# wk loaded in halves, and the last group's softmax sums on VectorE in fp32

## Chip, cores and metric

The kernel runs on one core of one Trainium2 chip. The metric is the device time of one execution in microseconds (us); for a kernel it is the median of several executions. The hardware profiler also took one execution apart, and all spans, durations and waits below come from that one.

## What is computed

A transformer block with conditioning, on 2048 rows of 512 features in bf16. Attention looks back at eight positions, every second one; the feed-forward part is gated by a GELU.

```python
mod = (silu(c) @ w_mod)                       # six vectors of 512: sa, ca, ga, sb, cb, gb
h = layernorm(x) * (1 + ca) + sa
q, k, v = split(h @ wqkv)                     # 32 heads of 16
idx = pos[:, None] - 2 * arange(8)[None, :]   # 8 keys behind each row; a negative index is masked
logits = einsum('bhsd,bhswd->bhsw', q, k[idx]) * 16 ** -0.5
attn = softmax(logits, axis=-1)               # over the 8 positions
o = einsum('bhsw,bhswd->bhsd', attn, v[idx])
x = x + ga * (o @ wo)
h = layernorm(x) * (1 + cb) + sb
x = x + gb * ((gelu(h @ w_gate) * (h @ w_up)) @ w_down)   # inner width 1792
```

## The kernel before

The 2048 rows are worked through in five groups (`GROUPS`): two of 256 rows and three of 512, numbered 0 to 4. Each group passes through `ln1` (first layer norm and its transposition into hT), `emit_qkv` (products with wq, wk, wv into PSUM, cast by ScalarE into qT, kT, vT), `emit_attention` and `emit_ffn`. The cast v rows are stored into a DRAM scratch (`scr`, L708) and read back in a layout with four shifted copies (`vR`, L725), because the sum over positions needs v by head and shift.

In attention a partition holds one head and one of four positions (128 = 4 x 32 heads), and an index `wg` of 2 in the free dimension makes eight of them. VectorE multiplies q with shifted k (`pq`, L764); TensorE folds the 16 features of a head into logits (`LT`, L776) with a 0/1 matrix. The maximum over the eight positions is taken by VectorE. For the groups 0 to 3 it is subtracted by a product (L824); for the group in `DVEMAX`, group 4, VectorE spreads it over the four partition quarters (L804) and subtracts it in fp32 in PSUM (L813). ScalarE writes the exponentials into `e` (L831). The sums over the eight positions come from two products with the matrix `F1` into a PSUM tile `ss` (L839): F1 adds the four quarters and puts the sum back into all four of them, and the two products add the two halves of e. ScalarE inverts the sum in place as exp(-ln(ss)) (L844, L845), and VectorE multiplies e by it (L848). Then come the products with vR (`pv`, L860 and L866), their fold into `o_ps` (L879), the projection with woP (`x_ps`, L904), the second layer norm, and the transposition into h2T, by DMA for all groups but group 0, followed by a modulation on ScalarE (L597).

The feed-forward part makes pairs of `g_ps` and `u_ps` (L945), 14 of them for a group of 512 rows, in a ring of four PSUM banks (`psF`) that the qkv and `y_ps` products share. ScalarE takes the GELU of the first (L954) and casts the second (L957), VectorE multiplies them (L958), and the products with WdP (`y_ps`, L971) are added to x on VectorE (L979) and stored by DMA (L982). The exponential and the GELU need different activation tables, and ScalarE loads one wherever its order changes from one to the other.

The order of the instructions is not that of the code. Each function hands its operations to a planner, `Plan`, with the engine, an estimated duration, what it reads and writes, and a priority `pri`. `Plan.order` places one operation after another: the key is the estimated start, padded by a margin of the engine (`MARGIN`) unless the engine is busy longer anyway, and among equal starts the priority decides. For loads `AHEAD` and `SKEW` stand for how far the DMA queue may run ahead and how late a transfer is seen. `emit` then issues everything in that order, so each engine works through a fixed queue. All loads, the transposing DMAs, the stores and the scr and vR transfers are issued on SyncE's (SP's) queue, in that same order. The key and the sort:

```python
if o.dma and o.pri > -996.9:
    at = max(at, pipe - self.AHEAD)
turn = self.TURN if o.eng == "pe" and o.cols != cols else 0.0
key = (max(free, at + self.MARGIN[o.eng]) + turn, o.pri)
```

The tag `prod`, six buffers, holds the pq and pv products; for the groups in `MERGE`, 3 and 4, three of the eight products lie in the buffers of wq, wk and wv. For group 0 the qkv products are cut along the contraction: wk is used in two cuts, feature blocks 0 and 1, then 2 and 3. wq is loaded in two DMAs, wk and wv in one each (L421).

Of the kernel before, what the change touches and what calls it, by code (L numbers as in the profile page):

```python
# [8 lines left out]
ACT = mybir.ActivationFunctionType  # L9
ALU = mybir.AluOpType  # L10
AX = mybir.AxisListType
F32 = mybir.dt.float32
# [6 lines left out]
def _ap(base, free_dims, offset=0):  # L19
    return bass.AP(base.tensor, base.offset + offset, [list(base.ap[0])] + [list(d) for d in free_dims])  # L20
# [164 lines left out]
class Engines:  # L185
    def __init__(self, nc, pl):
# [14 lines left out]
MERGE = (3, 4)  # L201
FMERGE = 0
DVEMAX = (4,)
CUT = 384
XB1 = {4: "act"}
XB2 = {1: "act", 2: "act", 3: "act", 4: "act"}
PRI = {
        "mod0": 3.1,
        "ln1": (-1825.3, -1417, -559.1, -142.2, 405),
        "qkv": (-441.8, 155.6, 232.8, 131.6, 1308),  # L210
        "att": (-554.3, 44.5, -1074.5, 462.1, 1752.4),
        "ffn": (1196.5, 2593, 2774.3, 2477.6, 1886.7),
        "glu": (5.6, 211.5, -2302.6, 838.6, 2147),
        "mod": (-159.3, -303.9, 262.1),
        "wo": 1823,
        "wd": 1171.4,
        "scr": -3307.9,
        "vR": -3609.4,
        "warm": (5, 6, 0, 3),
        "load": {"wk": -997.5, "wv": -995.5, "x1": -997.86, "x2": -995.23, "wm2": -1001.63, "wo": -878.5, "x3": -1000.04,  # L220
        "wm3": -994.66, "wm4": -996.59, "x4": -995.73, "Wg": -868.86, "Wu": -870.61, "wm5": -855.38, "Wd":
        -862.75},
}
Plan.MARGIN = {"pe": 0.48, "act": -0.15, "dve": 0.16, "pool": -1.48, "sp": 0.37}
Plan.AHEAD = 2.07
Plan.SKEW = 2.6
Plan.TURN = 0


# [1 line left out]
def kernel(  # L231
# [13 lines left out]
    nc = tc.nc  # L245
    P = 128
    S, D = 2048, 512
    H, DH, W = 32, 16, 8
    F = 1792
    SG = 512  # L250
    DT = D // P
# [22 lines left out]
    def ctile(shape, dtype, name):  # L274
        t = Tl(None, shape, dtype, name)
        t.t = const.tile(shape, dtype, name=name)
        return t

    T = pl.tile
    E = Engines(nc, pl)  # L280
    pe, act, dve, gp, dma = E.pe, E.act, E.dve, E.pool, E.dma
    MM = 0.2158

    def act_us(n, ptr=0):
        return 0.055 + n * 0.833e-3 + 0.093 * ptr
# [8 lines left out]
    F1 = ctile([P, P], BF16, "F1")  # L294
# [65 lines left out]
    wqkv = [T(t, [P, DT, D], BF16, t) for t in ("wq", "wk", "wv")]  # L360
    woP = T("woP", [P, 4, D], BF16, "woP")
    Wg = T("Wg", [P, DT, F], BF16, "Wg")
    Wu = T("Wu", [P, DT, F], BF16, "Wu")
    WdP = T("WdP", [P, FT, D], BF16, "WdP")
    kT = ctile([P, 4, ROW], BF16, "kT")
    scr = T("scr", [P, 4, ROW], BF16, "scr")

    def xrow(tok):
        ci = tok // P
        return xs[ci // 4][:, ci % 4, :]  # L370
# [12 lines left out]
    wm3 = T("h2T", [P, 4, D], BF16, "wm3")  # L383
    wm4 = T("h2T", [P, 4, D], BF16, "wm4")
    wm2 = [T("hh", [P, 2, D], BF16, "wm2", "early") for _ in range(2)]
    wm5 = [T("hh", [P, 2, D], BF16, "wm5", "early") for _ in range(2)]
# [17 lines left out]
    def load_rows(t, src, p, cuts, rows):  # L404
# [7 lines left out]
    L = PRI["load"]  # L412
# [3 lines left out]
        w=[wm01], pri=-999, bw=390e3)  # L416

    def load_wqkv(b, p, cuts=1):
        m = DT // cuts
        for i in range(cuts):  # L420
            dma(524e3 / cuts, lambda i=i: nc.sync.dma_start(  # L421
                out=wqkv[b][:, m * i:m * i + m, :],
                in_=A_wqkv[m * i * P:m * (i + 1) * P, b * D:(b + 1) * D].rearrange("(o p) n -> p o n", p=P)),
                w=[(wqkv[b], k) for k in range(m * i, m * i + m)], pri=p + 0.02 * i)

    load_wqkv(0, -998.65, 2)
    load_wqkv(1, L["wk"])
    load_wqkv(2, L["wv"])
    load_x(2, 4, L["x1"])
    load_x(4, 8, L["x2"])  # L430
# [1 line left out]
    for d4 in range(4):  # L432
        dma(131e3, lambda d4=d4: nc.sync.dma_start(  # L433
            out=woP[32 * d4:32 * d4 + 32, :, :],
            in_=bass.AP(A_wo.tensor, A_wo.offset + 4 * D * d4, [[16 * D, H], [D, 4], [1, D]])), w=[(woP, d4)],
            pri=L["wo"], bw=250e3)
# [31 lines left out]
    def sigmoid():  # L468
# [6 lines left out]
        w=[scT], pri=-2000)  # L475
# [72 lines left out]
    mod0 = []  # L548
# [108 lines left out]
    q, hT, vR = {}, {}, {}  # L657
# [56 lines left out]
    def emit_attention(g):  # L714
        tok0, n = GROUPS[g]
# [5 lines left out]
        for i, t in enumerate(vR[g]):  # L721
            rs = [(scr, (gg, i if GROUPS[gg][1] == SG else 0)) for gg in range(max(g - 1, 0), g + 1)]
            for r in (0, 2, 1, 3):
                queue, on = (nc.scalar, E.dma_act) if r in SECOND else (nc.sync, dma)
                on(32 * 4 * njv * (n + 8) * 2, lambda r=r, t=t, i=i, queue=queue: queue.dma_start(  # L725
                    out=t[32 * r:32 * r + 32, :, :, :].rearrange("p a b c -> p (a b) c") if njv == 4
                    else t[32 * r:32 * r + 32, :, :, :],
                    in_=bass.AP(scr.t.tensor, scr.t.offset + 2 * i * ROW + tok0 + 2 + 2 * r,
                                [[16 * ROW, H], [ROW, 16], [1, n + 8]] if njv == 4 else
                                [[16 * ROW, H], [4 * ROW, 4], [ROW, 2], [1, n + 8]])),  # L730
                    r=rs, w=[(t, r)], pri=PRI["vR"] + 0.1 * g, bw=330e3 if SECOND else 205e3)
# [8 lines left out]
        def kd(j):  # L740
            return kdep + [(kT, (bl, j)) for bl in blocks(tok0 - HALO, tok0 + n)]
# [15 lines left out]
        for jj in range(steps):  # L757
            p = base + jj
            pq = products("pq", jj)
            pqs.append(pq)  # L760
            for m in range(4):
                j, wg = (2 * jj + m // 2, m % 2) if n == SG else (m, 0)
                no = 4 if n == SG else 8
                dve(1.145, lambda j=j, wg=wg, no=no, t=pq[m]: nc.vector.tensor_tensor(  # L764
                    out=t[:], in0=_ap(q[g][:, j, :], [[0, no], [1, n]]),
                    in1=_ap(kT[:, j, :], [[2, no], [1, n]], offset=tok0 + HALO - (6 + 8 * wg if no == 4 else 14)),
                    op=ALU.mult), r=[(q[g], j)] + kd(j), w=[pq[m]], pri=p)
# [14 lines left out]
        p = base + 5  # L782
# [9 lines left out]
        e = T("e", [P, 2, n], BF16, "e")  # L792
        for b in range(nb):
            act(act_us(SG), lambda b=b: nc.scalar.copy(out=Lb[:] if nb == 1 else Lb[:, b:b + 1, :], in_=LT[b][:]),
                r=[LT[b]], w=[(Lb, b)], pri=p - 1000)
        us = 0.072 + n * 0.52e-3
        dve(us, lambda: nc.vector.tensor_tensor(out=Lb[:, 0, :], in0=Lb[:, 0, :], in1=Lb[:, 1, :], op=ALU.max),
            r=[Lb], w=[Lb], pri=p)
        if g in DVEMAX:
            mx = [T("ub", [P, n], BF16, "mx") for _ in range(2)]  # L800
# [11 lines left out]
            for b, t in enumerate(LT):  # L812
                dve(0.072 + SG * 2 // nb * 1.041e-3, lambda t=t: nc.vector.tensor_tensor(  # L813
                    out=t[:], in0=t[:], in1=_ap(all4[:], [[0, 2 // nb], [1, n]]), op=ALU.subtract), r=[t, all4], w=[t],
                    pri=p)
        else:
            dve(us, lambda: nc.vector.tensor_tensor(out=Lb[0:64, 1, :], in0=Lb[0:64, 0, :], in1=Lb[64:128, 0, :],
                                                    op=ALU.max), r=[Lb], w=[Lb], pri=p)
            dve(us, lambda: nc.vector.tensor_tensor(out=Lb[0:32, 0, :], in0=Lb[0:32, 1, :], in1=Lb[32:64, 1, :],
                                                    op=ALU.max), r=[Lb], w=[Lb], pri=p)  # L820
# [11 lines left out]

        act(act_us(SG) * nb, exps, r=LT, w=[e], pri=p - 1000, table="exp")

        ss = T("psB", [P, n], F32, "ss")

        def sums():
            for wg in range(2):
                nc.tensor.matmul(ss[:], lhsT=F1[:], rhs=e[:, wg, :], start=(wg == 0), stop=(wg == 1))  # L839

        pe(2 * MM * n / SG, sums, r=[F1, e], w=[ss], pri=p, pad=ss)

        def invert():
            nc.scalar.activation(out=ss[:], in_=ss[:], func=ACT.Ln)  # L844
            nc.scalar.activation(out=ss[:], in_=ss[:], func=ACT.Exp, scale=-1.0)  # L845

        act(2 * act_us(n) + 0.1, invert, r=[ss], w=[ss], pri=p - 1000, table="exp")
        dve(0.072 + 2 * n * 1.041e-3, lambda: nc.vector.tensor_tensor(  # L848
            out=e[:], in0=e[:], in1=_ap(ss[:], [[0, 2], [1, n]]), op=ALU.mult), r=[e, ss], w=[e], pri=p)

        oT = T("oT", [P, 4, SG], BF16, "oT")
        pvs = []
        for jj in range(steps):
            p = base + 6 + jj
            pv = products("pv", jj)
            pvs.append(pv)
            if n == SG:
                for m in range(4):
                    jl, wg = m // 2, m % 2
                    dve(1.145, lambda jj=jj, jl=jl, wg=wg, t=pv[m]: nc.vector.tensor_tensor(  # L860
                        out=t[:], in0=_ap(e[:, wg, :], [[0, 4], [1, n]]),
                        in1=vR[g][jj][:, :, jl, 8 - 8 * wg:8 - 8 * wg + n], op=ALU.mult),
                        r=[e, vR[g][jj]], w=[pv[m]], pri=p)
            else:
                for j in range(4):
                    dve(1.145, lambda j=j, t=pv[j]: nc.vector.tensor_tensor(  # L866
                        out=t[:].rearrange("p (w d) s -> p w d s", w=2), in0=_ap(e[:], [[n, 2], [0, 4], [1, n]]),
                        in1=_ap(vR[g][0][:], [[-8, 2], [njv * (n + 8), 4], [1, n]], offset=j * (n + 8) + 8),
                        op=ALU.mult), r=[e, vR[g][0]], w=[pv[j]], pri=p)

        for jj, pv in enumerate(joined(pvs)):
# [11 lines left out]
            for m, t in enumerate(o_ps):  # L883
                j = njv * jj + nj * m
                act(act_us(SG), lambda j=j, t=t: nc.scalar.copy(out=oT[:, j:j + nj, 0:n], in_=t[:]),
                    r=[t], w=[(oT, j)], pri=p - 1000)
        p = base + 11
# [3 lines left out]
        for half in range(n // 256):  # L891
# [5 lines left out]
            for i in range(2):  # L897
# [4 lines left out]
                def proj(c4=c4, x1_ps=x1_ps):  # L902
# [6 lines left out]
                    out=xrow(tok), in0=x1_ps[:], scalar=1.0, in1=xrow(tok), op0=ALU.mult, op1=ALU.add,  # L909
                    accum_out=sx[:, i:i + 1]), r=[x1_ps, xkey(tok)], w=[xkey(tok), (sx, i)], pri=p)  # L910
                act(0.7, lambda i=i, tok=tok, xn=xn, sq=sq: nc.scalar.activation(  # L911
                    out=xn[:, i, :], in_=xrow(tok), func=ACT.Square, scale=D ** -0.5, accum_out=sq[:, i:i + 1]),
                    r=[xkey(tok)], w=[(xn, i), (sq, i)], pri=p - 1000)
# [4 lines left out]
                out=rstd[:], in0=sx[:], scalar=-1.0, in1=sx[:], op0=ALU.mult, op1=ALU.mult), r=[sx], w=[rstd], pri=p2)  # L918
            dve(0.09, lambda sq=sq, rstd=rstd: nc.vector.scalar_tensor_tensor(  # L919
                out=rstd[:], in0=rstd[:], scalar=EPS, in1=sq[:], op0=ALU.add, op1=ALU.add), r=[sq, rstd], w=[rstd],  # L920
                pri=p2)
# [8 lines left out]
    def emit_ffn(g):  # L930
# [29 lines left out]
        for c4 in range(n // P):  # L960
            gc = tok0 // P + c4
            cuts = ((0, CUT), (CUT, D)) if gc == S // P - 1 else ((0, D),)
            for cut, (lo_d, hi_d) in enumerate(cuts):
# [21 lines left out]
    for g in range(NG):  # L985
        n = GROUPS[g][1]
        hT[g] = T("hT", [P, n // P, DT, P] if g in XB1 else [P, DT, n], BF16, "hT")
        ln1(g, hT[g], PRI["ln1"][g])
        if g == 0:
            mod_keep(mod0, -969)  # L990
            dve(0.34, lambda: nc.vector.tensor_copy(out=wide.t[:, 0, :].rearrange("p (t n) -> p t n", n=P),
                                                    in_=_ap(scT[:], [[1, 4], [0, P]])), r=[scT, hT[0]], w=[(wide, 0)],
                pri=-950)
        emit_qkv(g)
        if g == 0:
# [4 lines left out]
                                                       op=ALU.mult), r=[woP, (wide, 1)], w=[woP], pri=PRI["wo"])  # L1000
            for f0 in range(0, FT, 2):
                dve(0.6, lambda f0=f0: nc.vector.tensor_tensor(
                    out=WdP[:, f0:f0 + 2, :], in0=WdP[:, f0:f0 + 2, :], in1=_ap(gbB[:], [[0, 2], [1, D]]),
                    op=ALU.mult), r=[(WdP, f0), (WdP, f0 + 1), gbB], w=[(WdP, f0), (WdP, f0 + 1)], pri=PRI["wd"])
# [33 lines left out]
```

## Time and profile before

| what | value |
|---|---|
| device time, median of 5 | 243.84 us (242.17 to 244.07) |
| profiled execution, its own time | 243.5 us |
| its span, first to last instruction | 241.6 us |
| TensorE busy | 233.9 us, 1588 products |
| VectorE busy | 160.9 us |
| ScalarE busy | 159.3 us |
| GpSimd busy | 13.9 us |
| data moved by DMA | 28.23 MB |
| granted TensorE clock | 0.998 |

The busy time is per engine and the engines work side by side. PE is TensorE's multiplication, PEld its weight load, DVE is VectorE, ACT is ScalarE, POOL is GpSimd, and SPq is SyncE's queue of DMA issues. A row of a timeline gives the start, the duration, the engine, the line, the instruction with its output and inputs, and the count. A wait row gives who waited for whom, the total, how often, and the longest.

### The profile page before, as it was taken

What the parts mean: (1) busy time and instruction counts of PE and PEld (TensorE: products, weight loads), DVE (VectorE), ACT (ScalarE), POOL (GpSimd) and SP (SyncE); (2) the same over time, 40 slices, a digit from 0 to 9 for tenths busy, and PEclk for the clock granted to TensorE, in tenths of its full rate; (3) what the DMA queues carried; (4) which work ended last, traced back from release to release, by engine and by line L of the source; (5) the groups of instructions that cost most, each with busy time, mean ns of one, the idle gap of its engine ahead of it and who ended that gap; (6) DMA issues with size and microseconds to landing.
All of it is one profiled execution on the core that took longest, in us unless ns stands there. A gap on an engine that the chain in (4) does not pass through costs nothing.

```text
span 241.6 us, 4190 instructions
## 1 busy us (share of the span) xinstructions
PE 233.9 (97%) x1588; PEld 125.8 (52%) x1588; DVE 160.9 (67%) x307; ACT 159.3 (66%) x298; POOL 13.9 (6%) x35
## 2 busy tenths in 40 slices
PE   7899998999999999999999999999999999999994
PEld 2798544557674547765444444444444444444442
DVE  4689849849998699982799897589456222222222
ACT  4388785689786878579867676746867801666400
POOL 6000230000001000020000002000001000000000
PEclk9999999999999999999999999999999999999999
DMA  6999999999941129504118503200003110000011
GB/s 214 361 367 307 305 260 368 222 290 212 212 85 32 55 56 256 133 12 79 43 45 206 104 0 66 67 22 23 3 1 63 26 43 15 29 0 3 0 43 43
DMA packets 34917, 28.23 MB, mean 117 GB/s; under 512 B 10961, under 2 KB 33234, under 8 KB 34898
## 3 DMA queue, kind: packets, MB, share of 16 engines
q1 hardware_dynamic: 34896, 27.97, 46.1%
q8 instruction: 12, 0.20, 0.3%
q14 instruction: 7, 0.06, 0.1%
q10 hardware_dynamic: 2, 0.00, 0.0%
HBM read 21.40 MB, written 4.21 MB: 106 GB/s over the span
## 4 chain that ended last, share of the span: by engine, by line
PE 81%; SPq 7%; DMA 7%; DVE 2%; issue 1%; DVEq 0%
PE u_ps L945 20%; PE g_ps L945 20%; PE y_ps L971 20%; PE qkv_ps L681 8%; PE x_ps L904 6%; DMA vR<-scr 4%; DMA scr<-vT 3%; PE o_ps L879 3%; PE LT L776 3%; SPq L377 2%; DVE pv L866 1%; SPq L433 1%; SPq L395 1%; SPq L400 1%; SPq L725 1%
## 5 line engine op out<-in xcount | busy, mean ns | idle before, releaser
L945 PE MATMUL g_ps<-h2T,Wg 128*128 128x512 bf16 (+1 forms) x280 | 57.7, 337 | 0.0
L945 PE MATMUL u_ps<-h2T,Wu 128*128 128x512 bf16 (+1 forms) x280 | 57.7, 337 | 0.0
L971 PE MATMUL y_ps<-WdP,hht 128*128 128x512 bf16 (+2 forms) x238 | 50.4, 367 | 0.0
L954 ACT ACTIVATE gl<-g_ps 128x512 bf16<-128x512 f32 x56 | 33.5, 598 | 23.9 <-PE g_ps L945 19.0
L958 DVE TENSOR_TENSOR hht<-gl,ub 128x512 bf16<-128x512 bf16 x56 | 23.4, 422 | 31.0 <-ACT ub L957 30.8
L957 ACT CAST ub<-u_ps 128x512 bf16<-128x512 f32 x56 | 32.8, 585 | 15.7 <-PE u_ps L945 15.7
L945 PEld LDWEIGHTS <-Wg 128*128 128x128 bf16 x280 | 27.1, 98 | 23.3 <-issue 1.7
L945 PEld LDWEIGHTS <-Wu 128*128 128x128 bf16 x280 | 27.1, 98 | 22.2 <-issue 1.3
L764 DVE TENSOR_TENSOR pq<-qT,kT 128x2048 bf16<-128x2048 bf16 x32 | 38.0, 1217 | 0.9 <-ACT kT L704 0.9
L971 PEld LDWEIGHTS <-hht 128*128 128x128 bf16 x238 | 22.7, 98 | 25.8 <-issue 0.4
L860 DVE TENSOR_TENSOR pv<-e,vR 128x2048 bf16<-128x2048 bf16 x24 | 28.3, 1218 | 0.1
L979 DVE TENSOR_TENSOR x_sg<-y_ps,x_sg 128x512 bf16<-128x512 f32 (+2 forms) x17 | 10.8, 657 | 26.1 <-PE y_ps L971 26.1
L541 POOL TENSOR_TENSOR rstd<-rstd,neghalf 128x2 f32<-128x2 f32 x12 | 9.8, 820 | 169.5 <-DVE rstd L919 108.5
L681 PE MATMUL qkv_ps<-hT,wq 128*128 128x512 bf16 (+1 forms) x80 | 16.5, 336 | 0.7 <-ACT hT L551 0.6
L681 PE MATMUL qkv_ps<-hT,wk 128*128 128x512 bf16 (+1 forms) x80 | 16.4, 337 | 0.7 <-DMA wk<-in_A_wqkv_dram 0.7
L681 PE MATMUL qkv_ps<-hT,wv 128*128 128x512 bf16 (+1 forms) x80 | 15.5, 337 | 0.0
L904 PE MATMUL x_ps<-woP,oT 128*128 128x512 bf16 x64 | 15.3, 379 | 0.0
L911 ACT ACTIVATE xn<-x_sg 128x512 bf16<-128x512 bf16 x16 | 10.0, 627 | 4.2 <-DVE x_sg L908 4.0
L704 ACT CAST kT<-qkv_ps 128x512 bf16<-128x512 f32 x16 | 9.3, 590 | 4.4 <-PE qkv_ps L681 4.4
L620 DVE BATCH_NORM_STATS2 st<-x_sg 128x6 f32<-128x512 bf16 x16 | 10.2, 679 | 2.3 <-DMA x_sg<-in_A_x_dram 2.3
L681 PEld LDWEIGHTS <-wk 128*128 128x128 bf16 x80 | 8.7, 114 | 5.7 <-DMA wk<-in_A_wqkv_dram 1.0
L681 PEld LDWEIGHTS <-wq 128*128 128x128 bf16 x80 | 8.7, 113 | 5.3 <-issue 1.2
(100 smaller groups left out, 217.5 us busy)
## 6 DMA issues: line engine op xcount, KB each, us to landing
vR<-scr SPq DMA_DIRECT2D x24, 260.0 KB, 5.0
vR<-scr SPq DMA_DIRECT2D x8, 264.0 KB, 8.9
out_dram<-x_sg SPq DMA_DIRECT2D x15, 128.0 KB, 1.7
Wu<-in_B_w_up_dram SPq DMA_DIRECT2D x2, 896.0 KB, 10.5
scr<-vT SPq DMA_DIRECT2D x7, 256.0 KB, 7.4
Wg<-in_B_w_gate_dram SPq DMA_DIRECT2D x2, 896.0 KB, 7.8
WdP<-in_B_w_down_dram SPq DMA_DIRECT2D x2, 896.0 KB, 9.6
x_sg<-in_A_x_dram SPq DMA_DIRECT2D x3, 512.0 KB, 8.9
```

Source lines behind the costliest of these rows:

```text
L620: stats = lambda i=i, st=st, tok=tok: nc.vector.bn_stats(out=st[:, i, :], in_=xrow(tok + P * i))
L681: nc.tensor.matmul(shaped(ps[:, jl, :], g, XB1), lhsT=wqkv[b][:, dt, j + jl:D:4], rhs=columns(hT[g], g, dt, XB1), start=(dt == 0 and (jl = ...
L764: dve(1.145, lambda j=j, wg=wg, no=no, t=pq[m]: nc.vector.tensor_tensor(out=t[:], in0=_ap(q[g][:, j, :], [[0, no], [1, n]]), in1=_ap(kT[:, ...
L860: dve(1.145, lambda jj=jj, jl=jl, wg=wg, t=pv[m]: nc.vector.tensor_tensor(out=t[:], in0=_ap(e[:, wg, :], [[0, 4], [1, n]]), in1=vR[g][jj][ ...
L904: nc.tensor.matmul(x1_ps[:], lhsT=oT[:, j, c4 * P:(c4 + 1) * P], rhs=woP[:, j, :], start=(j == 0), stop=(j == 3))
L911: act(0.7, lambda i=i, tok=tok, xn=xn, sq=sq: nc.scalar.activation(out=xn[:, i, :], in_=xrow(tok), func=ACT.Square, scale=D ** -0.5, accum ...
L945: nc.tensor.matmul(shaped(ps[:, f, :], g, XB2), lhsT=Wt[:, dt, ft * P:(ft + 1) * P], rhs=columns(h2[g], g, dt, XB2), start=(dt == 0), stop ...
L954: act(act_us(SG), lambda gl=gl, ps=gu[0]: nc.scalar.activation(out=gl[:], in_=flat(ps), func=ACT.Gelu_apprx_tanh), r=[gu[0]], w=[gl], pri= ...
L957: act(act_us(SG), lambda ub=ub, ps=gu[1]: nc.scalar.copy(out=ub[:], in_=flat(ps)), r=[gu[1]], w=[ub], pri=p)
L958: dve(0.339, lambda gl=gl, ub=ub, ht=hh[u // 2], u=u: nc.vector.tensor_tensor(out=ht[:, u % 2, :], in0=gl[:], in1=ub[:], op=ALU.mult), r=[ ...
L971: nc.tensor.matmul(y_ps[:], lhsT=hh[u // 2][:, u % 2, f * n + c4 * P:f * n + (c4 + 1) * P], rhs=WdP[:, ft, lo_d:hi_d], start=(ft == 0), st ...
L979: dve(0.07 + nd * 1.041e-3, lambda y_row=y_row, y_ps=y_ps: nc.vector.tensor_tensor(out=y_row(), in0=y_ps[:], in1=y_row(), op=ALU.add), r=[ ...
```

## The change

wk is loaded by two DMAs of two feature blocks each, still as one operation of the planner. For group 4 (`DVESUM`) the two products into ss are replaced by fp32 additions on VectorE: s1 adds the two halves of e, s2 adds the upper 64 partitions to the lower 64, and four additions write the sum of both 32-partition halves of s2 to each quarter of s3. s1, s2 and s3 are fp32 tiles of the tag `prod` in SBUF. ScalarE inverts s3 in place, and e is multiplied by it. The other groups keep the products. The priorities, the margins, `AHEAD` and `SKEW` have new values.

```diff
 DVEMAX = (4,)
+DVESUM = (4,)
...
 PRI = {
-        "mod0": 3.1,
-        "ln1": (-1825.3, -1417, -559.1, -142.2, 405),
-        "qkv": (-441.8, 155.6, 232.8, 131.6, 1308),
-        "att": (-554.3, 44.5, -1074.5, 462.1, 1752.4),
-        "ffn": (1196.5, 2593, 2774.3, 2477.6, 1886.7),
-        "glu": (5.6, 211.5, -2302.6, 838.6, 2147),
-        "mod": (-159.3, -303.9, 262.1),
-        "wo": 1823,
-        "wd": 1171.4,
-        "scr": -3307.9,
-        "vR": -3609.4,
+        "mod0": 232,
+        "ln1": (-1746.8, -1408.1, -598.2, -71.1, 451.5),
+        "qkv": (-381.3, 137.8, 240.2, 131.6, 1324.9),
+        "att": (-554.3, 67.2, -1074.5, 592.2, 1636.2),
+        "ffn": (1214.9, 2614.9, 2774.3, 2238.4, 1956),
+        "glu": (-8.4, 214.5, -2060.3, 850.5, 2127.4),
+        "mod": (-285, -375.7, 388.4),
+        "wo": 1670.7,
+        "wd": 1130,
+        "scr": -3224.8,
+        "vR": -3489.3,
         "warm": (5, 6, 0, 3),
-        "load": {"wk": -997.5, "wv": -995.5, "x1": -997.86, "x2": -995.23, "wm2": -1001.63, "wo": -878.5, "x3": -1000.04,
-        "wm3": -994.66, "wm4": -996.59, "x4": -995.73, "Wg": -868.86, "Wu": -870.61, "wm5": -855.38, "Wd":
-        -862.75},
+        "load": {"wk": -997.5, "wv": -995.5, "x1": -997.86, "x2": -993.39, "wm2": -1001.63, "wo": -872.67, "x3":
+        -1000.04, "wm3": -989.07, "wm4": -995, "x4": -995.73, "Wg": -868.86, "Wu": -870.61, "wm5": -855.38,
+        "Wd": -862.75},
 }
-Plan.MARGIN = {"pe": 0.48, "act": -0.15, "dve": 0.16, "pool": -1.48, "sp": 0.37}
-Plan.AHEAD = 2.07
-Plan.SKEW = 2.6
+Plan.MARGIN = {"pe": 0.51, "act": -0.16, "dve": 0.22, "pool": -0.68, "sp": 0.23}
+Plan.AHEAD = 1.95
+Plan.SKEW = 2.48
...
-    load_wqkv(1, L["wk"])
+
+    def load_wk():
+        for i in range(2):
+            nc.sync.dma_start(out=wqkv[1][:, 2 * i:2 * i + 2, :],
+                              in_=A_wqkv[2 * i * P:2 * (i + 1) * P, D:2 * D].rearrange("(o p) n -> p o n", p=P))
+
+    dma(524e3, load_wk, w=[(wqkv[1], k) for k in range(DT)], pri=L["wk"])
...
+        if g in DVESUM:
+            add = lambda out, a, b: nc.vector.tensor_tensor(out=out, in0=a, in1=b, op=ALU.add)
+            s1, s2, s3 = [T("prod", [P, n], F32, "s%d" % k) for k in range(3)]
+
+            def spread_sums():
+                for r in range(4):
+                    add(s3[32 * r:32 * r + 32, :], s2[0:32, :], s2[32:64, :])
+
+            dve(0.6, lambda: add(s1[:], e[:, 0, :], e[:, 1, :]), r=[e], w=[s1], pri=p)
+            dve(0.6, lambda: add(s2[0:64, :], s1[0:64, :], s1[64:128, :]), r=[s1], w=[s2], pri=p)
+            dve(2.4, spread_sums, r=[s2], w=[s3], pri=p)
+
+            def invert():
+                nc.scalar.activation(out=s3[:], in_=s3[:], func=ACT.Ln)
+                nc.scalar.activation(out=s3[:], in_=s3[:], func=ACT.Exp, scale=-1.0)
+
+            act(2 * act_us(n) + 0.1, invert, r=[s3], w=[s3], pri=p - 1000, table="exp")
+            dve(0.072 + 2 * n * 1.041e-3, lambda: nc.vector.tensor_tensor(
+                out=e[:], in0=e[:], in1=_ap(s3[:], [[0, 2], [1, n]]), op=ALU.mult), r=[e, s3], w=[e], pri=p)
+        else:
...
```

More of the change, by code (lines that the diff above doesn't have):

```diff
@@ L833, in emit_attention @@
         act(act_us(SG) * nb, exps, r=LT, w=[e], pri=p - 1000, table="exp")
[L835 to L845, printed above, removed]
@@ L847, in emit_attention, with sums, invert @@
-        act(2 * act_us(n) + 0.1, invert, r=[ss], w=[ss], pri=p - 1000, table="exp")
-        dve(0.072 + 2 * n * 1.041e-3, lambda: nc.vector.tensor_tensor(
-            out=e[:], in0=e[:], in1=_ap(ss[:], [[0, 2], [1, n]]), op=ALU.mult), r=[e, ss], w=[e], pri=p)
+        if g in DVESUM:
[14 more added lines that the diff above has]
+        else:
+            ss = T("psB", [P, n], F32, "ss")
+            def sums():
+                for wg in range(2):
+                    nc.tensor.matmul(ss[:], lhsT=F1[:], rhs=e[:, wg, :], start=(wg == 0), stop=(wg == 1))
+            pe(2 * MM * n / SG, sums, r=[F1, e], w=[ss], pri=p, pad=ss)
+            def invert():
+                nc.scalar.activation(out=ss[:], in_=ss[:], func=ACT.Ln)
+                nc.scalar.activation(out=ss[:], in_=ss[:], func=ACT.Exp, scale=-1.0)
+            act(2 * act_us(n) + 0.1, invert, r=[ss], w=[ss], pri=p - 1000, table="exp")
+            dve(0.072 + 2 * n * 1.041e-3, lambda: nc.vector.tensor_tensor(
+                out=e[:], in0=e[:], in1=_ap(ss[:], [[0, 2], [1, n]]), op=ALU.mult), r=[e, ss], w=[e], pri=p)
```

## Prediction

> **What bounds the kernel now.** I read the page first, then busy time in stretches, then PE's waits, the chain of waits, and last the two places that the diff touches. The page has one row per engine, busy tenths in 40 slices, and the shares of the chain that ended last:
>
> ```profile
> PE   7899998999999999999999999999999999999994
> ...
> PE 81%; SPq 7%; DMA 7%; DVE 2%; issue 1%; DVEq 0%
> ```
>
> TensorE is full outside the first slices and carries 81% of the chain. The stretches (us, then busy us and instruction count of PE, PEld, DVE, ACT, POOL, the clock, DMA share, GB/s) say from where:
>
> ```profile
> 30.00:41.40 11.40, 9.88 (x67) 5.03 (x65) 7.78 (x12) 8.79 (x17) 2.40 (x2) 1.00 1.09 315
> 41.40:60.00 18.60, 18.59 (x159) 11.47 (x162) 14.32 (x23) 15.05 (x30) 0.69 (x1) 1.00 1.19 244
> 146.00:172.00 26.00, 26.00 (x151) 11.66 (x154) 20.82 (x33) 16.99 (x28) 1.32 (x2) 1.00 0.17 41
> 237.40:241.60 4.20, 1.09 (x16) 0.79 (x13) 1.40 (x3) 0.00 (x0) 0.00 (x0) 0.87 0.20 62
> ```
>
> From 41.4 to 237.4 us TensorE has no gap at full clock. So the time is a head of 41.4, TensorE's work behind it, and a tail of 4.2. DVE has 26 - 20.82 = 5.2 us free in the stretch with the last group's softmax. PE's waits before 41.5 us (total, times, longest):
>
> ```profile
> PE o_ps L879 <- DVE pv L866: 1.1, 2, 0.7
> PE qkv_ps L681 <- DMA wk<-in_A_wqkv_dram: 0.7, 1, 0.7
> PE qkv_ps L681 <- ACT hT L551: 0.6, 2, 0.4
> PE LT L824 <- DVE Lb L819: 0.4, 1, 0.4
> ```
>
> With two waits of 0.2 these are about 3 us, all that a better head could give after the start-up. The chain of waits (start, us, what) says what fixes the head's end:
>
> ```profile
> 16.17 0.53 SPq L433
> ...
> 16.83 8.10 DMA scr<-vT
> ...
> 27.39 9.16 DMA vR<-scr
> ...
> 40.14 1.23 DVE pv L866
> ...
> 41.41 0.40 PE o_ps L879 x8
> ```
>
> The v rows go to DRAM and back; the last pv product ends at 41.37 and releases the last fold into o_ps. That, not the early matmuls, starts the gapless stretch. The store at 16.83 stood behind two woP issues on SP's queue (to 16.70), while its last vT cast ended at 15.25 + 1.08 = 16.33.
>
> **What the Trainium skill says.** "VectorE: DVE Perf Modes", the section on the TRN2 errata, prices an fp32 tensor_tensor at (N+151)/0.96 ns, 691 at N = 512, and its tier table keeps fp32 at 1x. The trace agrees: the fp32 subtraction at L813 takes 694 ns, and L848 with 1024 elements 1214 against 1224. "TensorE: Matmul & The Clock Gate", Back-to-back issue gap, gives 518 cycles, 216 ns, for 512 columns; the two ss products take 0.43 on the chain. "DMA: Bandwidth & Descriptors", Queues, rings and completion order, says that descriptors are consumed in ring order on each DMA engine, so the first half of wk should land ahead of the second; the trace agrees as far as wk (issued 3.77, 6.8 to landing) precedes wv (4.28, 7.8).
>
> **The sums, part by part.** The parts now, from DVE's, PE's and ACT's timelines:
>
> ```profile
> 151.64 1.30 DVE L813 TENSOR_TENSOR LT<-LT,mx 128x512 f32<-128x512 f32 x2
> 155.62 0.59 PE L839 MATMUL ss<-e,F 128*128 128x512 bf16 x2
> 156.28 0.58 ACT L844 ACTIVATE ss<-ss 128x512 f32<-128x512 f32 x1
> 156.89 0.58 ACT L845 ACTIVATE ss<-ss 128x512 f32<-128x512 f32 x1
> 157.50 1.22 DVE L848 TENSOR_TENSOR e<-e,ss 128x1024 bf16<-128x1024 bf16 x1 [1.85 <-ACT ss L845]
> ```
>
> Removed: two products in the gapless stretch, 2 x 0.216 = **-0.43 us**, in full, since whatever stands behind them on PE moves up. A PSUM bank of psB comes free as well; PE never waits for one there, so nothing.
>
> Added on DVE: s1 on 128 partitions, s2 on 64, four additions on 32. Partitions do not shorten them: the max over 64 partitions takes 0.422 us, over 32 0.416. So 6 x 0.69 = 4.1 us, with overlap (the two at L813 span 1.30) some 4.0. Free DVE time there is 5.2 us, and 172 to 200 us holds 9.71 busy of 28. Ln and Exp read SBUF instead of PSUM; no row shows that on 512 fp32 elements, so 1.2 us with 0.2 either way. The last exp ends at 152.37 + 1.19 = 153.56. Then 4.0 of sums, 1.3 for the two y_ps additions (L979) that stand there, 1.2 for Ln and Exp: e is multiplied from about 160.1 instead of 157.5, **2.6 us later** (1.3 if the additions move behind). Queued behind on DVE are pv, hht and y additions; on ACT the gelu table load.
>
> Who waits? The chain to the last group's FFN: pv, o_ps at 171.7, x_ps, xn, two transposing DMAs, and the last h2T modulation ends at 190.94 + 2.22 = 193.2, before its first product at 197.7, in the middle of 56 y_ps products (190.1 to 203.9). So 4.5 us of slack as ordered, and some 9 if those products all go first. Cost of 2.6 us: nothing; without cover it is PE's time one for one.
>
> The gelu side: y_ps work of 12.1 us (56 x 0.216) starts at 147.9 and needs no gelu of group 3; it and two g/u pairs (four psF banks, 3.5 us) feed PE to 163.4. The first gelu must be done by then, so its table load (1.28 us in the trace) and gl (0.60) must start by 161.5. Inversion ends at 160.1. It fits by 1.4 us.
>
> The three prod buffers are of six; in group 4 pq and pv use only five per pass, the others lie in the finished wq, wk, wv. I find no new wait.
>
> wk: wk to wv is (4.28+7.8)-(3.77+6.8) = 1.51 us for 512 KB, so half of it lands 0.75 earlier, at 9.8, where the q products end. The four products of the first cut (0.11 each) then run during the wait, and the k products end 0.44 earlier; wv lands at 12.08 against its first product at 12.35, so 0.2 to 0.3 goes on. But the last fold still waits for pv: in the present order the gain falls into the 1.1 us of o_ps waits and nothing is left. I take **-0.2**, between -0.74 (whole wait, carried through) and +0.5 (the added issue, 0.47 to 0.51 us on SP, carried down SP's queue to the scr store). Against the latter: SP's issues from 4.84 on mostly take 0.7 to 2.4 us each, so SP is paced by DMA there, which moves the same bytes.
>
> The priorities: sorted, old and new lists of the compute stages have the same order but for mod0; the loads move wm4 alone, which must follow wm3 anyway. So the order changes by the margins, AHEAD, SKEW and the new costs, not by rank. I price it at 0, with both sides open.
>
> Sum against the profiled execution, 243.5 (span 241.6 and 1.9 around it): 243.5 - 0.43 - 0.2 = 242.9. The median of the five times is 243.84, 0.3 above it; from there **243.2**.
>
> **The rivals.** Something of about 0.5% (1.22 us) is what a measurement of this kernel can tell from no change; from 243.84 that is 242.62 and 245.06.
>
> Head re-timed for the better: the margins put the scr store ahead of a woP issue (SP's margin falls from 0.37 to 0.23) or other PE work into the waits. For: 3 us of waits stand in the head. Against: ranks are the same. Half of 2.6 us (o_ps, wk, hT; Lb is 0.4) and the 0.43: 243.84 - 1.3 - 0.43 = 242.1.
>
> Head re-timed for the worse, ending slower: the scr store falls behind one half of Wu, the next load on SP. 896 KB at 350 GB/s are 2.6 us, carried through scr, vR, pv to the fold at 41.4: 243.84 - 0.43 + 2.6 = 246.0. It decides when the store's planned time plus margin comes later than SP is free after woP; past 1.7 us of slip the result is slower than 245.06. For: vT was ready only 0.4 us before SP was. Against: the margin fell.
>
> Exp window too long: inversion past 161.5 stalls PE one for one. All four y additions and 0.2 of ACT put it at 161.7; a stall of 0.1 to 1 us: 243.5 to 244.4, no change.
>
> The change doesn't do its work: the k products wait for both halves, and the 0.43 alone stays: 243.4.
>
> **How the numbers follow.** Likeliest sum 0.42 (own range 242.6 to 243.9), halves useless 0.05, exp window 0.05 of which 0.02 slower; head better 0.31; head worse 0.17. Faster 0.31, same 0.50, slower 0.19. The range takes the likely sum and most of both head cases: 241.7 to 245.5.
>
> **What would show it.** Right: PE gapless from near 41 us, two fewer 512-column ss products, six fp32 additions of 0.69 each on DVE, gl after the inversion with no PE wait behind it, first k product near 9.9. Wrong: the last early o_ps fold far from 41.4, a PE wait on gl or hht between 155 and 200, fp32 additions of other length, or a span that moves by over 1.2 us with the head unmoved.

## The result, and the profile after

The changed kernel takes 243.73 us (median of 44 executions, 242.32 to 246.08) against 242.78 us for the kernel before (79 executions). The ratio is 1.0035, with a 95% interval of 1.0019 to 1.0050: slower by 0.46 to 1.2 us, where 0.6 faster was forecast. On a second occasion, beside variants of itself, it was 1.0003 (0.9971 to 1.0034), so the whole time alone does not settle whether the kernel got slower. The profiled execution took 243.74 us with a span of 241.8, 0.2 longer than the one before.

The page of the changed kernel, the same two rows as before:

```profile
PE   7899996999999999999999999989999999999994
...
PE 78%; DMA 9%; SPq 5%; DVE 4%; issue 2%; ACT 1%; DVEq 0%
```

Two digits changed. The 6 in the seventh slice, 36 to 42 us, was an 8: the head, where the waits for pv grew. The 8 in the 27th slice, 157 to 163 us, was a 9: TensorE has a gap where it had none, and ACT, absent from the chain before, carries 1% of it. The stretches (columns as before) put a size to the second:

```profile
41.40:60.00 18.60, 18.60 (x167) 11.54 (x163) 14.32 (x23) 15.23 (x30) 0.69 (x1) 1.00 1.17 249
146.00:172.00 26.00, 25.31 (x130) 11.26 (x122) 22.59 (x37) 17.03 (x27) 1.14 (x2) 1.00 0.17 41
```

PE is busy 25.31 us of 26; DVE rises from 20.82 to 22.59 and still has free time. PE's waits name the gap:

```profile
PE g_ps L972 <- ACT gl L981: 0.7, 1, 0.7
PE o_ps L906 <- DVE pv L893: 1.8, 3, 0.7
PE qkv_ps L688 <- DMA wv<-in_A_wqkv_dram: 0.3, 1, 0.3
```

The first row is new. The o_ps waits grew from 1.1 to 1.8, and the wait for wk, 0.7, became one of 0.3 for wv. The chain in the head (start, us, what):

```profile
17.19 7.23 DMA scr<-vT
...
26.44 9.88 DMA vR<-scr
...
39.96 1.23 DVE pv L893
...
41.23 0.40 PE o_ps L906 x8
```

The chain of the head is as before, and its end comes within 0.2 us of where it was. (The scr store is issued 0.36 us later than the 16.83 of before, and its transfer is 0.87 shorter.) The timelines of the last group's softmax on PE, DVE and ACT:

```profile
158.03 1.03 PE L972 MATMUL g_ps<-h2T,Wg 128*128 128x512 bf16 x4
158.90 1.03 PE L972 MATMUL u_ps<-h2T,Wu 128*128 128x512 bf16 x4
159.76 1.89 PE L998 MATMUL y_ps<-WdP,hht 128*128 128x512 bf16 x8
162.34 1.02 PE L972 MATMUL g_ps<-h2T,Wg 128*128 128x512 bf16 x4 [0.69 <-ACT gl L981]
```

```profile
153.49 0.69 DVE L1006 TENSOR_TENSOR x_sg<-y_ps,x_sg 128x512 bf16<-128x512 f32 x1 [0.76 <-PE y_ps L998]
154.09 0.68 DVE L843 TENSOR_TENSOR s<-e 128x512 f32<-128x512 bf16 x1
154.78 0.69 DVE L1006 TENSOR_TENSOR x_sg<-y_ps,x_sg 128x512 bf16<-128x512 f32 x1
155.50 3.55 DVE L843 TENSOR_TENSOR s<-s 64x512 f32<-64x512 f32 x5
160.41 1.23 DVE L859 TENSOR_TENSOR e<-e,s 128x1024 bf16<-128x1024 bf16 x1 [1.36 <-ACT s L856]
161.56 1.28 DVE L1006 TENSOR_TENSOR x_sg<-y_ps,x_sg 128x512 bf16<-128x512 f32 x2
```

```profile
159.09 0.63 ACT L855 ACTIVATE s<-s 128x512 f32<-128x512 f32 x1 [2.92 <-DVE s L843]
159.75 0.63 ACT L856 ACTIVATE s<-s 128x512 f32<-128x512 f32 x1
160.40 1.28 ACT L981 ACT_TABLE_LOAD   x1
161.69 0.60 ACT L981 ACTIVATE gl<-g_ps 128x512 bf16<-128x512 f32 x1
```

Read from the bottom: the inversion ends at 159.75 + 0.63 = 160.38, then the gelu table is loaded, then gl frees a psF bank at 162.29, and at 162.34 PE starts the next g product. Its work before that, eight y_ps products of 0.216 from 159.76, was through at 161.49. The wait row says 0.69 because the modelled end of a product reaches past the start of the next; from issue to issue the gap is 162.34 - 161.49 = 0.85.

Another release lies close by. The addition of the third y tile, which VectorE's order puts behind the multiplication of e and so behind the inversion too, ends near 161.56 + 0.69 = 162.25 and frees a bank as well. By the banks that the program assigns, the g product at 162.34 takes the bank of the first pair's g_ps, which gl alone frees; the bank of the third y tile goes to the u product at 163.20, which does not wait. So gl makes the gap, as the wait row says.

### The profile page after: what moved, and what is told of

Read it like the earlier page. It is cut to its first block, busy times and chain, and to the rows that moved or that the text cites. A ratio compares the mean times of both kernels' runs of the same rounds, so it can differ in the third digit from the quotient of the medians.

```text
span 241.8 us, 4197 instructions
## 1 busy us (share of the span) xinstructions
PE 233.7 (97%) x1586; PEld 125.5 (52%) x1586; DVE 164.5 (68%) x313; ACT 159.2 (66%) x298; POOL 12.9 (5%) x35
## 4 chain that ended last, share of the span: by engine, by line
PE 78%; DMA 9%; SPq 5%; DVE 4%; issue 2%; ACT 1%; DVEq 0%
PE g_ps L972 20%; PE u_ps L972 20%; PE y_ps L998 17%; PE qkv_ps L688 8%; PE x_ps L931 6%; DMA vR<-scr 4%; DMA scr<-vT 3%; PE o_ps L906 3%; PE LT L783 3%; DMA wm<-in_w_mod_dram 2%; DVE s L843 2%; SPq L440 1%; SPq L396 1%; DVE pv L893 1%; SPq L378 1%
## 5 line engine op out<-in xcount | busy, mean ns | idle before, releaser
L887 DVE TENSOR_TENSOR pv<-e,vR 128x2048 bf16<-128x2048 bf16 x24 | 28.5, 1219 | 0.1
L548 POOL TENSOR_TENSOR rstd<-rstd,neghalf 128x2 f32<-128x2 f32 x12 | 8.8, 740 | 174.2 <-DVE rstd L946 112.8
L604 ACT ACTIVATE h2T<-h2T,modT,scl 128x512 bf16<-128x512 bf16 (+1 forms) x16 | 10.9, 751 | 5.1 <-DMA h2T<-xn 5.1
L893 DVE TENSOR_TENSOR pv<-e,vR 128x2048 bf16<-128x2048 bf16 x8 | 9.3, 1219 | 4.1 <-DMA vR<-scr 4.0
L688 PEld LDWEIGHTS <-wv 128*128 128x128 bf16 x80 | 8.6, 114 | 5.8 <-issue 1.0
```

The costliest lines, as they stand in the source:

```text
L604: act(act_us(n, 2), lambda dt=dt: nc.scalar.activation(out=dst[:, :, dt, :], in_=dst[:, :, dt, :], func=ACT.Identity, scale=scl[:, off // ...
L688: nc.tensor.matmul(shaped(ps[:, jl, :], g, XB1), lhsT=wqkv[b][:, dt, j + jl:D:4], rhs=columns(hT[g], g, dt, XB1), start=(dt == 0 and (jl = ...
L893: dve(1.145, lambda j=j, t=pv[j]: nc.vector.tensor_tensor(out=t[:].rearrange("p (w d) s -> p w d s", w=2), in0=_ap(e[:], [[n, 2], [0, 4], ...
```

## The experiments

A measure that leaves the head out: from the start of the last early o_ps fold (the x8 row that ends the head) to the start of the last y addition. At full clock it is 237.42 - 41.41 = 196.01 us in the kernel before and 237.66 - 41.23 = 196.43 in the changed one. Theory A was that the exponential table's window is too long and makes the loss; the rivals were the added DMA issue (B), the new priorities and margins (C), and parts that work against each other (D).

**wk_only.** The kernel before, with the new load alone (`load_wk` as in the change):

```diff
-    load_wqkv(1, L["wk"])
+    dma(524e3, load_wk, w=[(wqkv[1], k) for k in range(DT)], pri=L["wk"])
```

> The kernel before with wk in two DMAs and nothing else; the order on every engine is that of before. Theory A (the exponential window: the fp32 sums keep ScalarE on the exponential table too long): this is without effect, 0.0 against before within 0.3 us, the first k product starts 0.7 us earlier and the last early o_ps fold still ends near 41.8. Theory B (the head got worse through the added DMA issue on SP): slower by up to 0.5 us, with the scr store issued 0.4 to 0.5 later. Theory C (new priorities and margins are to blame): 0.0.

Measured 0.9968 (0.9945 to 0.9990), 0.8 us faster, where theory A allowed 0.3. The stretch is 236.56 - 40.55 = 196.01, as before, so whatever is gained lies in the head. Its PE timeline:

```profile
9.79 1.94 PE L686 MATMUL qkv_ps<-hT,wk 128*128 128x256 bf16 x16
12.04 0.63 PE L686 MATMUL qkv_ps<-hT,wv 128*128 128x256 bf16 x4 [0.31 <-DMA wv<-in_A_wqkv_dram]
```

All sixteen k products run without a wait from 9.79 (10.58 before), and wv is late next. The scr store was issued at 16.36, not later than the 16.83 before. Over the profiles of all runs it stands between 16.25 and 18.13 in the ten with wk in halves and between 16.42 and 16.83 in the four with wk whole, with a median of 16.6 in both. B is not seen.

**sums_only.** The kernel before with the fp32 sums alone (the whole `DVESUM` branch of the change, of which the first lines stand here):

```diff
+        if g in DVESUM:
+            s1, s2, s3 = [T("prod", [P, n], F32, "s%d" % k) for k in range(3)]
```

> The kernel before with the fp32 sums on VectorE for group 4, old priorities and margins, wk whole. Theory A: PE waits for gl some 0.7 to 1.4 us near 162 and saves 0.43, so 0.3 to 0.9 slower than before, most of the whole change. Theories B and C: no wait on gl to speak of in a normal run, 0.43 faster than before.

Measured 1.0001 (0.9981 to 1.0020), an interval that holds both the loss of 0.42 us (0.17%) that the stretch shows and the gain of 0.43 that B and C expected. The stretch and the wait decide for A: 237.45 - 41.02 = 196.43, exactly that of the changed kernel, with the same wait on gl:

```profile
162.13 1.02 PE L967 MATMUL g_ps<-h2T,Wg 128*128 128x512 bf16 x4 [0.69 <-ACT gl L976]
```

**order_only.** The kernel before with the priorities, `AHEAD` and `SKEW` of the change and its margins:

```diff
-Plan.MARGIN = {"pe": 0.48, "act": -0.15, "dve": 0.16, "pool": -1.48, "sp": 0.37}
+Plan.MARGIN = {"pe": 0.51, "act": -0.16, "dve": 0.22, "pool": -0.68, "sp": 0.23}
```

> The kernel before with only the new priorities, margins, AHEAD and SKEW. Theory A: 0.0 within 0.3 us, no PE wait near 162. Theory C: 0.5 to 1.0 slower, and the lost time stands before 41 us or in new PE waits. Theory B: 0.0.

Measured 0.9995 (0.9968 to 1.0022), stretch 237.02 - 41.01 = 196.01. The new numbers move few of TensorE's 1588 products, and none of SP's issues. C is out behind the head, and with it as a cause of the gap; for the head the interval leaves room for up to 0.5 us.

**after_bf16.** The changed kernel with

```diff
-            s1, s2, s3 = [T("prod", [P, n], F32, "s%d" % k) for k in range(3)]
+            s1, s2, s3 = [T("prod", [P, n], BF16, "s%d" % k) for k in range(3)]
```

> The changed kernel with s1, s2 and s3 in bf16 instead of fp32; same order on all engines. The six additions should take 0.42 instead of 0.69 us, so that the inversion ends about 1.6 us earlier. Theory A: PE's wait on gl near 162 vanishes, 0.7 to 1.3 us faster than the changed kernel, so 0.4 faster than before up to equal. Theories B and C: at most 0.1 faster than the changed kernel, 0.8 slower than before.

Measured 0.9959 (0.9938 to 0.9980). Its ACT and PE timelines:

```profile
157.65 0.63 ACT L856 ACTIVATE s<-s 128x512 bf16<-128x512 bf16 x1
158.30 1.28 ACT L981 ACT_TABLE_LOAD   x1
159.60 0.60 ACT L981 ACTIVATE gl<-g_ps 128x512 bf16<-128x512 f32 x1
```

```profile
159.21 1.67 PE L998 MATMUL y_ps<-WdP,hht 128*128 128x512 bf16 x7
160.72 1.03 PE L972 MATMUL g_ps<-h2T,Wg 128*128 128x512 bf16 x4
```

gl ends at 160.20, before the y_ps products do, and the gap is gone. (Counted from the LT fold the inversion ends 1.33 us earlier, not 1.6: a y addition between the sums waits 0.27 for PE.) The stretch is 236.04 - 40.47 = 195.57: the 0.43 of the two ss products, kept whole. The changed kernel lies 0.86 above it.

**after_again, after_no_sums, after_no_wk, after_bf16_again**: the changed kernel and three variants side by side. The edits, in this order: none; `DVESUM = ()`; wk in one DMA; the bf16 tiles again.

> The changed kernel as it is, beside its parts on one chip. The parts alone gave wk 0.9968, sums 1.0001, order 0.9995; if they add up, the whole is near 0.997 of before, and the ratio 1.0035 came from the chips or the executions it was taken on. If the parts work against each other (theory D), it is 1.0035 here too. In both cases PE waits about 0.7 us for gl near 162.

> The changed kernel with the sums of group 4 made by products again (wk in halves and the new order stay). Theory A: no PE wait on gl, two ss products of 0.43 us more; 0.26 us faster than the changed kernel where the wait is 0.69, more if the wait is longer in other executions. Theory D in wk and order: as slow as the changed kernel.

> The changed kernel with wk in one DMA. Prediction's sum: 0 to 0.4 us slower than the changed kernel. wk_only against before says 0.8 slower. Theory B (wk costs in the new order): faster than the changed kernel by 0.5.

> The changed kernel with bf16 sums, in direct comparison with the changed kernel. Theory A as visible in the profile: 0.69 us (0.3%) faster than it, no PE wait on gl. If it is much more than 0.7 us faster, the profile's wait does not tell the whole effect.

Measured, with the stretch of each:

| kernel | ratio to before | interval | stretch, us |
|---|---|---|---|
| after_again | 1.0003 | 0.9971 to 1.0034 | 196.44 |
| after_no_sums | 0.9980 | 0.9952 to 1.0007 | 196.02 |
| after_no_wk | 1.0008 | 0.9982 to 1.0033 | 196.44 |
| after_bf16_again | 0.9960 | 0.9934 to 0.9987 | 195.59 |

The stretch takes three values only, by how the sums are made: products 196.01, fp32 on VectorE 196.43, bf16 on VectorE 195.58. So behind the head the parts do not work against each other, and D is out there. The whole times scatter by the head besides: the three parts alone multiply to 0.9964, and the whole gave 1.0003, which the stretch does not explain. Without the sums the stretch is 0.42 shorter, where 0.26 was expected from the wait row of 0.69; the gap from issue to issue, 0.85 less 0.43, is the better measure. The bf16 version was expected 0.3% below the changed kernel and came out 0.43% below (0.9960 against 1.0003); the intervals hold both, and the stretch says 0.85 us, 0.35%.

**sums_longer and sums_s12_bf16.** The dose of the delay:

```diff
-                for r in range(4):
+                for r in (0, 0, 1, 2, 3):
```

> The changed kernel with one of the four spreading additions made twice, otherwise the same order and result. Theory A with one-for-one price: inversion ends 0.7 us later, PE's gap before the second g product of the pair grows from 0.85 to 1.55, and the stretch from the last early o_ps fold to the last y addition grows from 196.43 to 197.15 us. If the gap's length is set by something else (the y additions that free the other banks), the stretch stays at 196.4.

```diff
-            s1, s2, s3 = [T("prod", [P, n], F32, "s%d" % k) for k in range(3)]
+            s1, s2, s3 = [T("prod", [P, n], dt, "s%d" % k) for k, dt in enumerate((BF16, BF16, F32))]
```

> The changed kernel with s1 and s2 in bf16 and s3 in fp32. Two additions drop from 0.69 to 0.42, so the inversion ends 0.54 us earlier; Theory A: the gap shrinks to 0.3, the stretch to 195.9 us, between 196.43 of the changed kernel and 195.58 with all three in bf16.

Each of the two ran once, in 246.68 and 245.33 us, at a lower granted clock between 41 and 60 us (0.91), so only a stretch is read from them. It goes from the start of the group 4 LT fold, at full clock, to the start of the last y addition: changed kernel 237.66 - 144.96 = 92.70, longer 240.72 - 147.30 = 93.42, mixed 239.22 - 146.79 = 92.43, all bf16 236.04 - 144.19 = 91.85. PE's wait rows, first of the longer and then of the mixed kernel:

```profile
PE g_ps L972 <- ACT gl L981: 1.4, 1, 1.4
```

```profile
PE g_ps L972 <- ACT gl L981: 0.4, 1, 0.4
```

An addition of 0.71 us more costs 0.72: one for one. (It delays VectorE's y additions as much as gl, so this run alone does not tell the two releases apart; the banks do.) The mixed kernel gained 0.27 where 0.54 was expected. Its DVE timeline says why:

```profile
155.93 0.41 DVE L843 TENSOR_TENSOR s<-e 128x512 bf16<-128x512 bf16 x1
156.61 0.69 DVE L1006 TENSOR_TENSOR x_sg<-y_ps,x_sg 128x512 bf16<-128x512 f32 x1 [0.27 <-PE y_ps L998]
157.33 3.29 DVE L843 TENSOR_TENSOR s<-s 64x512 bf16<-64x512 bf16 x5
```

s1 is done 0.27 earlier, but the next instruction in DVE's queue is a y addition that waits for PE just so long. Only s2's saving came through.

**bf16_old_order.** wk in halves and bf16 sums (the rest of the `DVESUM` branch as in the change) under the old priorities:

```diff
-    load_wqkv(1, L["wk"])
+    dma(524e3, load_wk, w=[(wqkv[1], k) for k in range(DT)], pri=L["wk"])
...
+            s1, s2, s3 = [T("prod", [P, n], BF16, "s%d" % k) for k in range(3)]
```

> The kernel before with wk in halves and bf16 sums on VectorE for group 4, old priorities and margins. Theory A: stretch 195.58 us and no gap, so 0.43 us faster than before behind the head, and with what wk gives in the head 0.4 to 1.2 faster in all: 0.995 to 0.998 of before.

Measured 0.9954 (0.9934 to 0.9974), stretch 237.35 - 41.77 = 195.58. It is faster than the kernel before, as are the two bf16 runs in the new order, and its stretch is 0.85 shorter than that of the changed kernel.

**costs_true.** The changed kernel, fp32 sums kept, other costs for the planner:

```diff
-            dve(0.6, lambda: add(s1[:], e[:, 0, :], e[:, 1, :]), r=[e], w=[s1], pri=p)
-            dve(0.6, lambda: add(s2[0:64, :], s1[0:64, :], s1[64:128, :]), r=[s1], w=[s2], pri=p)
-            dve(2.4, spread_sums, r=[s2], w=[s3], pri=p)
+            dve(0.69, lambda: add(s1[:], e[:, 0, :], e[:, 1, :]), r=[e], w=[s1], pri=p)
+            dve(0.71, lambda: add(s2[0:64, :], s1[0:64, :], s1[64:128, :]), r=[s1], w=[s2], pri=p)
+            dve(2.85, spread_sums, r=[s2], w=[s3], pri=p)
...
-            act(2 * act_us(n) + 0.1, invert, r=[s3], w=[s3], pri=p - 1000, table="exp")
+            act(2 * act_us(n) + 0.33, invert, r=[s3], w=[s3], pri=p - 1000, table="exp")
```

> The changed kernel, fp32 sums kept, with the planner told what they take on the chip: 0.69, 0.71 and 2.85 us instead of 0.6, 0.6 and 2.4, and 0.23 more for the inversion. The planner then puts one GELU of group 3, with two table loads around it, between the exponentials and the inversion, and orders a g/u pair of TensorE earlier. If the gap came from the planner's low costs, PE has no wait on gl and the stretch from the last early o_ps fold to the last y addition is 195.6 us, 0.85 less than in the changed kernel. If fp32 sums can't be covered here, or the two loads of 1.28 us cost as much, the stretch stays at or over 196.4.

Measured 0.9973 (0.9949 to 0.9998). From the LT fold to the last y addition (the clock was 0.91 between 41 and 60 us here too) it takes 238.55 - 146.70 = 91.85 us, as with bf16 sums, and PE waits for no gl. Its ACT timeline:

```profile
157.93 1.28 ACT L981 ACT_TABLE_LOAD   x1
160.84 0.60 ACT L981 ACTIVATE gl<-g_ps 128x512 bf16<-128x512 f32 x1 [1.63 <-PE g_ps L972]
161.46 1.28 ACT L263 ACT_TABLE_LOAD   x1
162.75 0.63 ACT L855 ACTIVATE s<-s 128x512 f32<-128x512 f32 x1
```

ScalarE stood idle while the sums were made; two table loads more, with one gl between them, free the bank in time. The inversion ends at 164.04, and costs nothing behind it. The new costs also put both y additions ahead of the multiplication of e, and reorder some of TensorE's products behind 180 us, where it has no gap in either kernel.

## Why the prediction was wrong, point by point

**The sign turned on one term: the cover of the gelu side.** The prediction let the y_ps work and two g/u pairs feed PE to 163.4 and had the inversion fit by 1.4 us. The mechanism was among its rivals, the chance (0.05) and the deciding point (161.5) were wrong. Two banks were counted as free that were not: while PE works on the first pair, the two last y tiles are unfinished and hold the other two psF banks. Two more products finish the third tile and six the fourth, at 161.49, and both banks then stay taken until VectorE has added them, from 161.56 on. So one pair fits, not two, and gl of that pair must be through when y_ps ends. The trace of the kernel before already had PE in that order, one pair, then eight y_ps products, then the next pair:

```profile
158.65 1.03 PE L945 MATMUL g_ps<-h2T,Wg 128*128 128x512 bf16 x4
159.51 1.03 PE L945 MATMUL u_ps<-h2T,Wu 128*128 128x512 bf16 x4
160.37 1.89 PE L971 MATMUL y_ps<-WdP,hht 128*128 128x512 bf16 x8
162.10 1.03 PE L945 MATMUL g_ps<-h2T,Wg 128*128 128x512 bf16 x4
```

Counted back, 161.49 less 0.60 for gl, 1.28 for the table and some 0.08 around them, the inversion had to end by 159.53; it ended at 160.38, close to the 160.1 that was forecast. The difference is the gap of 0.85. After 0.43 of gain, that is 0.42 of loss, which the stretches of the eleven profiles at full clock bear out to within 0.02; sums_longer and costs_true show the cause, the one by lengthening the chain, the other by taking the gelu out of its shadow while the fp32 sums stay.

**The range** of 241.7 to 245.5 holds the measured 243.73, but that says little for the account behind it: it was that wide for a better or worse head, and what came was the gap that had been given 0.05.

**The saving of 0.43** was right: 195.58 against 196.01 once the gap is away. **The additions** were right to 0.2 us: 0.68 each, and 0.68 + 3.55 = 4.23 for all six against the 4.0 that counted on some overlap, which these do not show (0.71 from one to the next). That the chain to the last group's FFN has slack was right too, since costs_true with a still later inversion loses nothing. But free time on an operation's own engine does not yet hide it. DVE had that time; ScalarE, which waited for DVE, held the exponential table meanwhile, and TensorE needed the gelu.

**wk.** The mechanism was as told: the k products start at 9.84 instead of 10.58, the wait moves to wv (0.3), whose products start 0.25 earlier (12.10 against 12.35), as forecast, and the o_ps waits grow from 1.1 to 1.8. The step was sized too low, 0.74 instead of 0.44, since the second half was there too when it was needed: the halves were issued at 3.7 and 4.2 and landed 6.1 to 6.3 us later, in order. In the profiles no gain reaches the end of the head: the last early o_ps fold starts at 41.3 in the median of the ten with wk in halves, at 41.0 in that of the four with wk whole. What wk is worth in the whole time stays open: 0.9968 for wk_only, but 1.0003 with it and 1.0008 without it in the new order. The head scatters by more than that: in the profiles shown the last early o_ps fold starts between 40.47 and 42.30, and in sums_only, where every instruction of the head stands in the order of before, it starts 0.39 earlier than in the profile before.

**The priorities** at 0 was right behind the head (196.01). A slip without weight: the waits named for a better head (o_ps, wk, hT) sum to 2.4, not 2.6, which makes that rival 242.2 instead of 242.1.

**The sum** of what the trace shows is +0.42 us behind the head. The first comparison's interval begins at 0.46 and centres on 0.85; the second (1.0003) centres on 0.07. So the gap explains half of the first difference at its centre. The trace does not show where the other 0.4 would have gone; it isn't in any wait of TensorE after 43 us, and the head's scatter is large enough for it. Its cause stays open.

## What to carry to other kernels

When work is moved from a full engine to a free one, follow what the slower path keeps occupied on the way, here the activation table, and count the buffers that the full engine still has then: banks held by unfinished accumulations are not cover. Measure such a change from a point behind the scattering part of the run, since a stretch that repeats to 0.02 us decides what the medians of 22 to 44 executions leave open; it says nothing of what the change does to the head. And give a hand-built planner measured costs: 0.65 us too little on the sums and 0.23 on the inversion decided between a loss of 0.42 and a gain of 0.43.

## What the runs showed of the hardware

An addition over 32 or 64 partitions takes as long as over 128: 680 to 687 ns in fp32 (the changed kernel), 414 to 420 in bf16 (after_bf16), for 512 elements. Ln and Exp on 512 elements take 0.63 us from SBUF, in fp32 and bf16 alike, against 0.58 in PSUM. The multiplication of e took 0.69 us with s3 in bf16 and 1.23 with it in fp32, so a scratch in bf16 also shortens the next instruction by 0.5; with the fp32 ss in PSUM it took 1.22, so against the kernel before nothing was lost there.
